# Another order and other buffers for a fused attention and feed-forward block: the feature map's table as the second transfer, its mask first on VectorE, a k weight product ahead of the first transposes

## The chip, the cores and the metric

The kernel runs on one core of one Trainium2 chip. The metric is the time of one execution on the device in microseconds (us). A core has a matrix engine (TensorE, PE in the profile; its weight loads are listed as PEld), three engines for element-wise work (VectorE or DVE, ScalarE or ACT, GpSimd or POOL), and SyncE (SP), which here only issues transfers between the chip's large memory and the on-chip buffers. Each engine takes its instructions strictly in the order in which they were issued to it; engines wait for one another by semaphores.

## What is computed

The input x has 2048 rows of 512. It is normalised, and goes into two branches: linear attention with 32 heads of 16 columns, whose feature map is a product per head followed by a softmax of p and of -p; and a dense layer of 1792, Mish, and a dense layer back. The result is x plus the product of the branches.

```python
def _A_ref(x, wqkv, w_phi, wo):
    ...
    pq = jnp.einsum("bhsd,hdf->bhsf", q, w_phi)
    pk = jnp.einsum("bhsd,hdf->bhsf", k, w_phi)
    phi_q = jnp.concatenate([_softmax(pq, axis=-1), _softmax(-pq, axis=-1)], axis=-1)
    phi_k = jnp.concatenate([_softmax(pk, axis=-1), _softmax(-pk, axis=-1)], axis=-1)
    kv = jnp.einsum("bhsf,bhsd->bhfd", phi_k, v)
    z  = jnp.einsum("bhsf->bhf", phi_k)
    num = jnp.einsum("bhqf,bhfd->bhqd", phi_q, kv)
    den = jnp.einsum("bhqf,bhf->bhq", phi_q, z)[..., None] + 1e-6
    o = num / den
    return (lambda x, *d: x.transpose(*d))(o, 0, 2, 1, 3).reshape(B, S, D) @ wo
...
xn = _layernorm(x, axis=-1)
s = _A_ref(xn, A_wqkv, A_w_phi, A_wo)
g = _silu(_B_ref(xn, B_w1, B_b1, B_w2))
return x + s * g
```

## The kernel before, in words

**Tiles.** The rows of x are cut into 16 tiles of 128 rows, called x0 to x15. `norm` (line 349 and on) loads a tile, takes its mean and variance, raises the variance to the power -1/2 on GpSimd (the result is `rs`), normalises the tile in place, and transposes it on TensorE into a PSUM bank `pt` by four products with the identity. Mean and variance come from VectorE's batch-norm instructions in tiles 0, 1, 4 and 5, and from two passes on ScalarE (the tile is only read, the output goes to a scratch `dev`) in the others.

**Precision.** All large products are made from operands split in two: a high half rounded to the matrix engine's format (`...h`, a copy on ScalarE) and the rest (`...l`, a subtraction on VectorE or GpSimd). A product is three matmuls: high by low, low by high, high by high. Products of weights by tiles are combined by sums of blocks (`sums_x`, `weights_s`, `sums1`), as in fast matrix multiplication, so that seven block products do the work of eight.

**The feature map** is folded into the weights of q and k. Its table `phic` (32 KB) is loaded once; a mask on VectorE spreads it into `phit`, a block-diagonal operand of four 128x128 blocks, and `folded` multiplies each 128 rows of the k weights (loads `wkT00`, `wkT01`, `wkT10`, `wkT11`) and q weights (`wqT..`) by it, four products for each. The products' names are `wkf00` to `wkf11` and `wqf00` to `wqf11`; `wkh`, `wkl` and `wkr` are the halves and a plain copy of a k weight product.

**Stages.** The tiles are normalised and multiplied by the k and v weights (`kx`, `ky`, `kz`, `v`), the softmax of k is taken and summed against v into the bank `kvp`; the first dense layer is the products `fx`, `fy`, `fz` (and `fxq`, `fyq`, `fzq` for q); then the attention's denominators (`tz`), numerators (`pn`) and output (`pw`); then the second dense layer (`x`, `y`, `z`, with Mish on `r`), the products with `md` and `me` last; at the end each tile of the result is put together (`final`) and stored.

**The order is written out by hand.** The functions don't issue instructions; they add them to a list of 2085 operations, numbered as they come (an operation is one instruction, or a group that stays together, such as the four products of `folded`). `Program.issue` then goes through the string `SCHED` and issues them in that order. A letter behind a number chooses the engine where an operation has versions for several: V for VectorE, G for GpSimd, A for ScalarE. The order matters only within each engine's queue, and between instructions that share a buffer. All transfers go to SP's queue, but for the first one in `SCHED`, which ScalarE issues:

```python
g = self.eng["A" if first and m == "dma_start" else e]
first = first and m != "dma_start"
getattr(g, m)(*a, **k)
```

**Buffers.** The string `PLACE` gives each of 985 tiles the number of its buffer within its pool: `slot` (38 large ones), `s2` (15 of 2 KB a partition), `ps` (8 PSUM banks), and small ones. A tile that follows another in the same buffer waits until the last reader of the one before is done; for a load this wait holds SP's queue.

**Numbers used below.** Operations 0 to 10 are eleven products of ones by ones, `wake`, which keep TensorE busy. 25, 155, 36, 366, 168, 240, 64, 379 and 114 load x0, x2, x4, x9, x6, x7, x1, x13 and x5. 11 loads `phic` and 12 is its mask. 13, 14, 15, 16 load `wkT00`, `wkT01`, `wkT10`, `wkT11`, and 17, 21, 56, 60 are the products `wkf00`, `wkf01`, `wkf10`, `wkf11`; 19, 23, 58 and 62 take the low halves of these four, and 63 the copy `wkr1` of the last. 26 to 31 are x0's statistics and normalisation (29 is GpSimd's power), 32 its transposes (`pt0`), 33 and 34 the halves of the result; 37 to 43 are the same for x4, with 42 the normalisation and 43 the transposes (`pt4`). 75 and 76 are the first products `k0`. 107 writes a column of ones. 721, 728 load q weights; 86 and 89 load the v weights. All of them are issued in line 194, so that the profile's groups are told apart by tiles, not by lines.

Of the kernel before, what the change touches and what calls it, by code (L numbers as in the profile page):

```python
# [55 lines left out]
394V 178 733 125V 179 218 395G 137G 389 90 91G 217 735V 219 376 96 353 734A 73 128V 97 253V 377 300 122 98A 143 220 126  # L56
127G 144 93 145 94 134G 221 301 302 186 396 187G 79 390 250 138 194V 99 101 129 123 256V 35 286 287 288 289 251 108 228
95A 109 81 222 146V 147 135 92A 290 130 229 223A 110A 303 230 224 100 78 80 82 131V 136G 262 263A 149 208A 254 304 231V
291 102 225 83 226 255V 139G 190 140G 191A 491 265 193 391 103 112 113G 292 267A 568 523 52 279 148 257 150 104 151 84
85 105 305 306 293 106 195A 258 141 307A 294A 264 192 207 53G 569 281A 210 152 167 188 447 74 142G 196 295 211 308 212  # L60
132 397 570 227 180 613 55 259G 261 197 209V 153 268 296 154 297 321 269 312A 54 189 572 573 313 198 524 525 200 199
448G 309 314G 479 322 452 333 316 354G 315G 450G 356G 357G 651 436 46 480 270 323 334A 336 335 201 202 203 492 493 310
527 338A 311 378 435 398G 351A 232 204 205 503 233 206 271 482 235 273 483 528 355G 484 451G 433 133 260 399 214 213
282 339 284 283 317 318G 285 494A 272 571 504A 656 506 495 274 324V 340 401 234 508A 280A 275 236 341 402 276 298 252
237 496 319 277 497 498 481 238 278 342 358 359G 652G 574 520 522A 413 350 352A 360 414A 505 415 499 416 449G 403 418A
# [36 lines left out]
1426 1577 1198 1199A 1251 1196 1348 1611 1477 1302A 1117 1305A 1259 1457 1260A 1162 1333 1334 1350 1461 1372 1201 1509
1303 1549 1202A 1682 1203 1197 1118 1276 1306 1505 1261 1478 1467 1281 1283 1279 1252 1351 1494 1238 1335 1369 1253
1254 1352 1255 1353 1472 1468 1277 1298 1256 1284 1354 1336 1355 1282 1280 1583 1601 1278 1337 1388 1338 1356 1357 1339
1672 1499 1569G 1683 1673 1340 1385 1257A 1258 1551 1661 1299A 1389A 1511 1662 1376 1534 1674 1550 1663 1584 1684 1386V
1685 1585 1552V 1686 1377 1379 1383 1664 1380 1675 1375 1543 1384 1378 1409 1693 1483 1390 1526 1387 1300 1535G 1469G
1447G 1412 1536G 1687 1665 1676 1440 1381 1688 1382 1436 1200 1677 1473 1474 1520 1553G 1554G 1666 1578 1579 1475 1410V
# [3 lines left out]
1470 1481 1482 1497 1538G 1544 1545 1540V 1603G 1604G 1606G 1506 1635 1501 1594 1507 1765 1525 1529 1502V 1556 1530  # L111
# [832 lines left out]
```

## Time and profile before

| | before |
|---|---|
| timed runs | 485.92 us median of 3 (485.03, 485.92, 491.89) |
| profiled execution, its own time | 484.66 us |
| its span, first to last instruction | 482.9 us |
| mean granted TensorE clock | 0.998 |
| moved by transfers | 112.96 MB, 234 GB/s over the span |

The profile is of one execution. Its span is the time between the first and the last instruction; the own time of the execution is 1.8 us longer. A row of a timeline gives the start, the length, the engine, the line, the operation with output and inputs, and in brackets the idle time before it and what ended that. "xN" counts instructions that were merged into one row; the length of such a row reaches from the first start to the last end. Matmuls are pipelined: a row's last matmul ends later than the next one starts, so that a rate is read from the starts. A product of 32-bit operands appears as two passes, so the four products of `folded` are eight entries.

### The profile page before, as it was taken

Reading aid. Unit: us, or ns where it says so; the run is one execution under the profiler, and the core shown is the slowest. Engines: PE = TensorE matmul, PEld = TensorE weight load, DVE = VectorE, ACT = ScalarE, POOL = GpSimd, SP = SyncE. Lnnn points to the kernel's source line nnn. Section 1 sums busy time; section 2 is a strip of 40 time slices with the busy share of each in tenths; the row PEclk is TensorE's granted clock in tenths of the full one; section 3 lists DMA queues with packets and bytes.
Section 4 is the critical chain, followed back from the end, with each engine's and each line's share of the span. In section 5 each row is a group of like instructions: output and inputs, shape, how many; then the busy total and the mean of one; then the engine's idle time right before and its main releaser. Section 6 shows DMA issues by size and latency. Waiting matters only on the chain.

```text
span 482.9 us, 9043 instructions
## 1 busy us (share of the span) xinstructions
PE 472.5 (98%) x3308; PEld 384.1 (80%) x3308; DVE 444.5 (92%) x749; ACT 316.2 (65%) x534; POOL 248.2 (51%) x168
## 2 busy tenths in 40 slices
PE   6999999999999999999999999999999999999995
PEld 6988888878888888887888877777888888888884
DVE  4999989987999999999999999998899957799985
ACT  6998866754334344435557576598988889976522
POOL 2899948504410084627833365019792627662430
PEclk9999999999999999999999999999999999999999
DMA  8815999674995057994685989985584567621476
GB/s 317 303 37 169 371 331 317 233 260 178 301 342 186 5 185 262 383 297 153 204 282 168 357 325 341 354 306 182 184 260 177 188 210 258 210 102 52 130 244 193
DMA packets 67004, 112.96 MB, mean 234 GB/s; under 512 B 5136, under 2 KB 37520, under 8 KB 66960
## 3 DMA queue, kind: packets, MB, share of 16 engines
q1 hardware_dynamic: 66816, 112.13, 68.6%
q8 instruction: 26, 0.43, 0.3%
q10 hardware_dynamic: 144, 0.26, 0.1%
q14 instruction: 18, 0.15, 0.1%
HBM read 74.62 MB, written 37.75 MB: 233 GB/s over the span
## 4 chain that ended last, share of the span: by engine, by line
PE 97%; DMA 1%; DVE 1%; ACT 1%; issue 0%; POOL 0%; DVEq 0%; ACTq 0%
PE fx L194 16%; PE x L194 16%; PE pw L194 9%; PE kx L194 8%; PE fy L194 8%; PE y L194 8%; PE fxq L194 5%; PE ky L194 4%; PE z L194 4%; PE fz L194 4%; PE kvp L194 2%; PE fyq L194 2%; PE kz L194 2%; PE pn L194 2%; PE pt L194 2%; PE k L194 1%
## 5 line engine op out<-in xcount | busy, mean ns | idle before, releaser
L194 ACT ACTIVATE r<-r,b1t 128x512 f32<-128x512 f32 x56 | 38.9, 717 | 0.6 <-DMA r<-hd 0.6
L194 POOL TENSOR_TENSOR w1al<-w1a,w1ah 128x768 fp32r<-128x768 f32 x9 | 16.8, 1862 | 33.3 <-ACT w1ah L194 31.1
L194 POOL TENSOR_TENSOR w1sl<-w1s,w1sh 128x1024 fp32r<-128x1024 f32 x9 | 21.6, 2411 | 22.7 <-PE kx L194 13.7
L194 POOL TENSOR_TENSOR mt<-r,r 128x512 f32<-128x512 f32 x9 | 13.7, 1522 | 32.8 <-ACT oh L194 18.6
L194 POOL TENSOR_TENSOR t<-r,mt 128x512 f32<-128x512 f32 x9 | 14.9, 1667 | 18.4 <-DVE u L194 12.3
L194 POOL TENSOR_TENSOR rs<-rs,mhalf 128x1 f32<-128x1 f32 x16 | 9.4, 598 | 20.3 <-DVE rs L194 16.5
L194 DVE TENSOR_REDUCE tz<-ez 128x64 f32<-128x1024 f32 x16 | 19.5, 1219 | 0.3
L194 POOL TENSOR_TENSOR tl<-ts,th 128x1024 fp32r<-128x1024 f32 x7 | 16.9, 2416 | 2.4 <-ACT th L194 2.4
L194 ACT ACTIVATE fz<-fx 128x512 f32<-128x512 f32 x14 | 8.2, 582 | 14.9 <-DVE v L194 8.1
L194 PE MATMUL kx<-wss,th 128*128 128x512 f32 x56 | 17.6, 396 | 0.0
L194 POOL TENSOR_TENSOR w1s<-w1a 128x256 f32<-128x256 f32 x16 | 11.9, 748 | 9.7 <-PE fy L194 6.8
L194 ACT ACTIVATE u<-h 128x512 f32<-128x512 f32 x12 | 7.0, 597 | 14.1 <-DVE h L194 14.1
L194 ACT ACTIVATE hd<-fx 128x512 f32<-128x512 f32 x12 | 7.1, 595 | 13.3 <-PE fx L194 13.0
L194 ACT ACTIVATE hc<-fx 128x512 f32<-128x512 f32 x12 | 7.2, 598 | 12.2 <-PE fx L194 12.1
L194 ACT ACT_TABLE_LOAD x11 | 14.1, 1283 | 1.4 <-PEq L936 1.2
L194 POOL TENSOR_TENSOR mt<-r,mt 128x512 f32<-128x512 f32 x9 | 14.8, 1645 | 0.4 <-ACT r L194 0.2
L194 ACT ACTIVATE ha<-fz 128x512 f32<-128x512 f32 x13 | 7.6, 595 | 10.6 <-PE fz L194 5.9
L194 POOL TENSOR_TENSOR md<-t,md 128x512 fp32r<-128x512 f32 x5 | 7.8, 1569 | 11.8 <-ACT md L194 11.8
L194 ACT ACTIVATE hb<-fx 128x512 f32<-128x512 f32 x14 | 8.2, 593 | 8.2 <-PE fx L194 8.2
L194 PE MATMUL pt<-ident,x 128*128 128x128 f32 x64 | 9.9, 287 | 3.2 <-DVE st L194 3.1
L194 PE MATMUL pw<-oh,wo0l 128*128 128x512 f32 x32 | 12.8, 399 | 0.0
L194 PE MATMUL pw<-ol,wo0h 128*128 128x512 f32 x32 | 12.5, 390 | 0.0
(1038 smaller groups left out, 1928.5 us busy)
## 6 DMA issues: line engine op xcount, KB each, us to landing
r<-hd SPq DMA_DIRECT2D x28, 512.0 KB, 5.0
scr<-xT SPq DMA_DIRECT2D x8, 512.0 KB, 6.6
scrT<-th SPq DMA_DIRECT2D x8, 512.0 KB, 7.0
scrT<-tl SPq DMA_DIRECT2D x8, 512.0 KB, 6.3
so<-so SPq DMA_DIRECT2D x16, 256.0 KB, 4.0
sr<-so SPq DMA_DIRECT2D x16, 256.0 KB, 4.5
xx<-xt SPq DMA_DIRECT2D x16, 256.0 KB, 4.1
x<-x SPq DMA_DIRECT2D x15, 256.0 KB, 4.1
```

What stands on the lines that cost most here:

```text
L194: getattr(g, m)(*a, **k)
```

## The change

Only the two strings `SCHED` and `PLACE` change. Every operation is kept, and three get another engine: 42, the normalisation of x4 (ScalarE to VectorE), 107, a column of ones (ScalarE to VectorE), and 1756, the low half `md3l` (GpSimd to VectorE).

At the start, by queue:

| queue | before | after |
|---|---|---|
| transfers | x0 (by ScalarE); SP: x2, x9, wkT11, phic, x4, x7, x6, x1, wkT00, wkT01, x13, wqT00, wqT01, x5, wqT10, wkT10, wv | x2 (by ScalarE); SP: x0, phic, wkT11, x9, x4, wkT10, x6, x7, wkT00, x1, x13, wkT01, wqT00, wqT10, x5, wqT01, wv |
| PE | 6 wake, pt0, wkf11, 3 wake, pt4, 2 wake, wkf00, wkf01, pt2, wqf00, pt6, wqf10, wkf10, pt1, wqf01, k0 | 6 wake, wkf11, pt0, wkf10, 3 wake, pt4, 2 wake, wkf00, pt2, wkf01, wqf00, wqf10, pt6, wqf01, pt1, k0 |
| VectorE | x0 statistics, rs0, x0 normalised, (x9), mask, (x9, x2), x4 statistics, rs4, wkr1, ... | x0 bn_stats, mask, (x2), bn_aggr, rs0, x0 normalised, (x9), x4 statistics, rs4, (x2, x9), wkr1, (x6, x2), x4 normalised, ... |
| ScalarE | x2, x9, x2, x9, xT0 high half, x7, x6, x4 normalised, wkf11 high half, ... | x2, x2, x9, x9, x6, xT0 high half, wkf11 high half, x7, ... |

On VectorE the low halves 19, 23 and 58 of k weight products each go ahead of other work, and the normalisations of x7 and x13 come behind 23 and 58. On GpSimd the sum `ws2` of weights goes ahead of `ws0`.

Behind that, TensorE's queue has two moves: 928 (a product of `fx10`) goes ahead of 774, and 1691 (a product of `x0_0`) ahead of 1703. Some 40 instructions of the other queues move by a few places. At the end, on SP, the store 2072 of a quarter of tile 11 goes ahead of the store 2022 of tile 12, and the two halves of tile 10 change places.

Of the 985 tiles most get another buffer number, but 76 follow another tile than before in their buffer; about half of these lie in the head, up to the first k and v products. Those that hold a load: wkT10 has a buffer of its own (before: behind wkT11), wkT01 follows the scratch of x2's passes (before: its own), x13 follows phic (before: its own), x5 follows x0 (before: phic), and x10 follows wkT00 (before: wkT01).

```diff
--- before.py
+++ after.py
@@ -48,76 +48,76 @@
 SCHED = """
-25 26 27 28 29 155 156 157 0 1 2 3 4 5 30 31V 32 366 367 159 16 11 368 12 36 370 369 158 33 37 160 371 38 39 40 41 60 6
-7 8 240 168 64 13 14 63V 379 241 169 161 162 170 42A 61 172 372 242 65 171 34 43 9 10 17 243 163V 21 164 720 721 114
-728 722 47A 244 15 48 66 173 174 67 62 18 380 175 373 245 176V 68 24A 107A 20A 724A 69 382 115 49G 381 51 19 116 177
-383 723A 181A 22 730 56 57 165 44 732A 374A 246 50G 384 70V 385 247 117 89 86 248V 23 386 387V 184G 118 71 725 727A
-731A 58 166 478 215 75 729 76 299 59V 119 182 45 77V 726V 183V 388 249 375 111G 87 88G 120A 121 392A 393 185 72 216
...
+155 25 26 11 156 12 157 159 27 28 29 30 31V 0 1 2 3 4 5 16 60 366 367 368 32 36 15 56 37 38 39 40 370 158 168 169 33
+371 63V 369 41 240 171 160 6 7 8 42V 43 13 64 379 14 161 170 34 65 162 61 241 242 172 720 728 372 9 10 243 163V 17 114
+164 47A 244 721 48 66 173 174 107V 67 62 380 18 175 373 245 176V 68 20A 21 24A 381 383 722 724A 382 69 19 49G 51 115
+723A 22 730 177 181A 57 165 44 732A 374A 246 50G 384 70V 116 385 247 89 86 23 117 386 248V 58 387V 184G 118 725 71 727A
+731A 166 478 215 75 729 76 299 59V 119 182 45 77V 726V 183V 388 375 87 137G 111G 88G 120A 733 121 392A 393 185 72 216
...
-880 888 774 777 980 887 928 1035 1060 842 1018 929A 881 782 889 1061 1036 1062 1064 882 930 783 890 852G 853 1019 1037
...
+819G 922 833 877 771 834 950 750 797 946 947 977G 925 940 941 927 747 966 923A 926A 928 929A 879 835 978 1016 886 979
...
-1732 1670 1746 1716 1717 1712G 1718 1738 1733 1719 1720 1721 1681 1692 1703 1691 1714 1747 1723V 1725 1702 1713 1724
+1732 1670 1716 1717 1712G 1718 1746 1738 1733 1719 1720 1721 1681 1692 1691 1747 1723V 1703 1714 1725 1702 1713 1724
...
-1742G 1735G 1878 1801 1766 1767 1760 1796V 1790 1768 1726 1802 1869 1820 1756G 1761 1728 1772 1850 1900 1862 1797 1839
+1742G 1735G 1878 1801 1766 1767 1760 1796V 1790 1768 1726 1802 1869 1820 1756V 1761 1728 1772 1850 1900 1862 1797 1839
...
-2050 1981 2023 2018 2024 2045G 1978 2019 2020 2025 2026 2068 2010 2016 2051 1985 2027 2028 2065 2034 2066 2081 2082
-1986 2073 2069 2077 2070 2083 2084 2074 2021 2075 2022 2071 2078 2079 2080 2072 2076 2037 2040 2043 2046 2049 2052 2053
-2056 2057 2054 2055 2058 2059
+2050 1981 2018 2023 2024 2045G 1978 2019 2020 2025 1985 2026 2068 2010 2016 2051 2027 2028 2065 2034 2066 2081 2082
+1986 2073 2069 2077 2070 2083 2084 2074 2021 2075 2071 2072 2022 2078 2079 2080 2076 2037 2040 2043 2046 2049 2056 2057
+2052 2053 2058 2059 2054 2055
 """
 PLACE = """
-0 6 7 3 12 13 5 5 9 8 11 4 5 0 0 0 1 0 2 1 8 7 3 8 14 9 3 4 6 17 20 1 2 7 1 2 11 13 6 15 23 19 4 5 10 3 5 16 20 21 15
...
+0 2 4 3 13 3 9 5 9 8 11 5 7 1 1 0 2 0 3 2 8 4 3 5 14 8 4 9 6 17 19 1 2 7 3 1 14 13 5 15 24 20 0 7 3 3 4 16 19 22 15 27
...
```

More of the change, by code (lines that the diff above doesn't have):

```diff
@@ L56 @@
[L56 to L65, printed above, removed]
@@ new lines @@
+93 145 94 134G 221 186 396 187G 79 390 250 138 194V 99 123 101 129 256V 35 286 287 288 289 251 108 228 95A 300 301 302
+109 81 222 146V 147 135 92A 130 229 223A 110A 303 230 224 100 78 290 80 225 82 131V 136G 262 263A 149 208A 254 304 231V
+291 102 83 226 255V 139G 190 140G 191A 491 265 193 391 103 112 113G 292 267A 568 523 52 279 148 257 150 104 151 84 85
+105 305 306 293 106 195A 258 141 307A 294A 264 192 207 53G 569 281A 210 152 167 188 447 74 142G 196 295 211 308 212 132
+397 570 227 180 613 55 259G 261 197 209V 153 268 296 154 297 321 269 312A 54 189 572 573 313 198 524 525 200 199 448G
@@ new lines @@
+309 314G 479 322 452 333 316 354G 315G 450G 356G 357G 651 436 46 480 270 323 334A 336 335 201 202 203 492 493 310 527
+338A 311 378 435 398G 351A 232 204 205 503 233 206 271 482 235 273 483 528 355G 484 451G 433 133 260 399 214 213 282
+339 284 283 317 318G 285 494A 272 571 504A 656 506 495 274 324V 340 401 234 508A 280A 275 236 341 402 276 298 252 237
+496 319 277 497 498 481 238 574 575 278 342 358 359G 652G 520 522A 413 350 352A 360 414A 505 415 499 416 449G 403 418A
+266A 509 454 529 430 526 344 239 343 510 654G 345 500 325 419 511 653G 453G 655G 434 530 124 549 658 445 442 444 362
@@ new lines @@
+364 441 327 326 657G 363 365 404A 420 659G 614 615 501 789 421 617 432A 328 502 660 400 406 405 455G 661 346 407 616
+347 348 550 662 551 552 408 663A 329 460 361G 330 331 337V 555 438 664 443 576A 553A 417A 409 461 665 521V 349 422 485
+618 332 619 486V 760V 620 556A 531A 465 462 759V 463A 457 487 459 456 532 554 423 425 410 458 424 411 533 558 666A 466A
+559A 668 446 440 437 507A 464 320 426 439 562 621A 488 536A 669V 412 431A 468 672 537 427 673A 469A 622 538V 540 489
+545 546 577 578 472 467 626V 539V 534 535 627 629G 579 563V 628V 470 630 541 542G 473A 631 623 632G 580 490 564 761V
@@ L76 @@
+639 640 475 476 512 557 624 428 429 581 667 692 582 583 641 513 515 514 516 670 560 633 634 693A 593 695 471 543 477
+625 678 786G 785G 762G 517 584A 586 518 519 642A 644 585 646 643 587 645 787G 788G 791 594A 595 675 647 790G 676 588
+680 589 544 596 565 648 548 547 635 636 598V 599 610 694 566 590 591 679 681 688 686 697A 709 612V 698 699 649 736 600
+592 650 700 611V 737 687 690 684 689 685 861 792G 765 738 862 863 701 601 603 605 602 703 604 864 739A 711A 606 865
 866A 696A 597A 638 713 637 712 702 741 953 704 705 607 608 955 706 609 952 710V 707 793 868 867 742A 869A 743 954 677
@@ L77 @@
 691 872 683 682 870 871 708 794 798 799A 744 956 745A 986 987 988 873 989 714 957 958 715 716 717 719 718 801 746 756
-994 996 995 990 991 758A 754A 992 763 874 751 875 876 752 755 764G 800 748 961 757V 802V 795 805 767 997 806A 749V 803
-960 963 820 811 1002G 766G 813G 1003 962 804 671 753 943 938 740 561 768 998 772 993 999 1004 1005 1001 964 821 816 769
+994 996 995 990 991 758A 754A 992 763 874 751 875 876 752 755 764G 800 748 961 757V 802V 795 805 767 997 806A 803 749V
+960 963 820 811 1002G 766G 813G 1003 962 804 671 753 943 938 561 768 998 772 993 999 1004 1005 1001 964 821 816 769
@@ L95 @@
-1230G 1244 1421A 1418A 1392 1329 1092 1107 1156 1186 1396 1361A 1532 1322 1314 1157 1342 1096 1341 1187 1397A 1033
+775 776A 828A 920 840 921 779 826 831 809 674 740 807 567 796A 780A 818 1010 841 829 1013 1014 830 832 885 878 1015
+819G 922 833 877 771 834 950 750 797 946 947 977G 925 940 941 927 747 966 923A 926A 928 929A 879 835 978 1016 886 979
+1137 1262 1017 880 888 774 777 980 887 1035 1060 842 1018 881 782 889 1061 1036 1062 1064 882 930 783 890 852G 853 1019
+1037 932 1039 1063 1038 949 843 902G 948 924 945 951 1065A 883 981 982 845 983 854 935 933A 1267 891 892 984 855 903
@@ new lines @@
+884 904 844 847 856 1086 846 1040A 781 810 944 942 474 1051 931 784 1067 1042 1119 1043A 1046 1120 1139G 1138G 1268G
+905 1263G 1140G 911G 1141G 857 959 858 985 906 1085 1047 1068A 848 1124 1071 1125A 1127 1142 1128A 1052G 907 908 849
+909 912 936 913 1088 1087 1121 910 1122A 1123 1265G 1264G 1143G 1054G 1126 1131 1132A 1056 778 934 1147 1072 914 1146
+915 1320 1144 1089 1145G 1266G 1269 1057G 1066 1041 1044 859 1069 1045 1271 1048 1073 1204 916 1129 1148 1149 1049 917
+1150 1074 1050 1130 1134 1135 1151 1205 1316 937 1133 1163 1053G 1075 918 1209 1055G 1058 1136 1566 1321 1272 1164 1165
@@ new lines @@
+1059G 1273 1206 1210A 1166A 1207A 1270G 1285 1222 1239 1324 1223 919 1274A 1240 1325 893G 968G 1326 1168 1169A 1241 894
+1224 850 895 1225 969 1212 1152 1171 1286A 1288 1317 1213A 1216 1211 896 970 1153 1172A 971 1327 1226 1567 1217A 1182
+851 1242 972 1175 1070 1170 1287 1176A 1289A 1292 1090 1091 1318 1184 1181 1167 1311 1310 1313 1319 1243 1328 1415 1173
+1214 1183 973 1219 897 1103 1290 1105 974 898 1178 975 1102 1177 1220 899 1179 1416 1295 1420 1358 1154G 1032 1312 1315
+1275 1093G 1323 1180 1293A 1568 1185 1294 1221 1359 900 1417 1391 1360 1363 1155 1227 1104 1106 1174 1094 1296 1095
@@ L96 @@
+1230G 1244 1421A 1342 1418A 1392 1329 1092 1107 1156 1186 1396 1361A 1532 1322 1314 1157 1096 1341 1187 1397A 1033
 1189G 1393 1394A 1097 1343 1098 1229 1344 1158 1398 1423 1419 1218 1362 1020 1215 1208 1399 1228 1424A 1400A 1345 1364A
@@ L98 @@
 1404A 1488 1110G 1291 1108 1476 1425 976 1406 1233 1407 1076 1111 1234 1112 1081 1082 1430 1431 1235 1370 1077 1083
-1079 1365 1084 1113 1078 1236 1021 1371A 1465 1023 1034G 1349G 1332G 1080 1114 1368 1346 1237 1190 1030 1489 1026 1456
+1079 1365 1084 1113 1078 1236 1021 1371A 1465 1023 1349G 1332G 1034G 1080 1114 1368 1346 1237 1190 1030 1489 1026 1456
 1022G 1455 1027 1031 1024 1450 1191 1429 1660 1395 1432 1402 1443 1297 1498 1373 1307 1247G 1248 1192 1246 1028 1249
 1115 1250 1374 1029 1193 1533 1445 1444 1330 1446 1347 1466 1116 1025 1194 1101 1195 1301 1304 1308A 1600 1671 1649
[L102 to L105, printed above, removed]
+1426 1577 1198 1199A 1251 1348 1611 1477 1302A 1117 1305A 1259 1457 1260A 1162 1333 1334 1196 1350 1461 1372 1201 1509
+1303 1549 1467 1202A 1682 1203 1197 1118 1276 1306 1505 1478 1281 1283 1279 1252 1351 1494 1261 1238 1335 1369 1352
+1253 1254 1255 1353 1472 1468 1277 1298 1256 1284 1354 1336 1355 1282 1280 1583 1601 1278 1337 1388 1338 1356 1357 1339
+1672 1534 1499 1569G 1683 1673 1340 1385 1257A 1258 1551 1661 1299A 1389A 1511 1662 1376 1674 1550 1663 1584 1684 1386V
 1685 1585 1552V 1686 1377 1379 1383 1664 1380 1675 1375 1543 1384 1378 1409 1693 1483 1390 1526 1387 1300 1535G 1469G
-1447G 1412 1536G 1687 1665 1676 1440 1381 1688 1382 1436 1200 1677 1473 1474 1520 1553G 1554G 1666 1578 1579 1475 1410V
+1447G 1412 1536G 1687 1665 1553G 1676 1440 1381 1688 1382 1436 1200 1677 1473 1474 1520 1554G 1666 1578 1579 1475 1410V
 1462 1650 1651 1413V 1414 1634 1612 1441 1463 1464 1613 1523 1580 1652 1437A 1521A 1451 1571V 1570G 1572G 1442 1653
```

26 lines of the change are left out of this document (2 added, 24 removed), and 40 rows, old and new, of the table PLACE.

## The prediction

> **What bounds the kernel now.** I read the page first: the busy times and the chain that ended last.
>
> ```profile
> span 482.9 us, 9043 instructions
> PE 472.5 (98%) x3308; PEld 384.1 (80%) x3308; DVE 444.5 (92%) x749; ACT 316.2 (65%) x534; POOL 248.2 (51%) x168
> ...
> PE 97%; DMA 1%; DVE 1%; ACT 1%; issue 0%; POOL 0%; DVEq 0%; ACTq 0%
> ```
>
> TensorE (PE) is busy for 472.5 of 482.9 us and carries 97% of the chain. The change neither removes nor adds a matmul, so all that it can win lies in the 10.4 us in which PE stands still. Next the view of what PE waited for, longest first, and the table by stage (after the length of the stage: PE, weight loads, DVE, ACT, POOL).
>
> ```profile
> PE pt L194 <- DVE st L194: 3.1, 1, 3.1
> PE wake L194 <- DVE mhalf L276: 1.1, 1, 1.1
> PE fx L194 <- issue: 1.0, 1, 1.0
> ```
>
> ```profile
> 11.00:18.50 7.50, 7.50 (x69) 7.43 (x68) 7.50 (x29) 7.50 (x21) 5.09 (x8) 1.00 1.02 361
> 18.50:30.00 11.50, 11.50 (x64) 9.67 (x64) 11.47 (x30) 11.47 (x25) 11.07 (x7) 1.00 0.40 137
> 30.00:478.00 448.00, 446.81 (x3149) 360.78 (x3148) 419.15 (x666) 289.68 (x475) 228.74 (x142) 1.00 0.69 234
> 478.00:483.00 5.00, 0.00 (x0) 0.00 (x0) 1.43 (x4) 0.58 (x2) 0.00 (x0) 0.80 0.36 100
> ```
>
> From 30 to 478 us PE stands still for 448.00 - 446.81 = 1.2 us, of which 1.0 is the one stop of fx that no engine explains ("issue"). The last 5 us have no matmul. The prize is the head, where the first tile's transposes wait 3.1 us.
>
> **The head, row by row.** The PE timeline (start, length, operation; the idle time before it in brackets), and one piece of the chain with eight passes further on:
>
> ```profile
> 1.12 2.93 PE L194 MATMUL wake<-ones 128*128 128x128 f32 x12 [1.12 <-DVE mhalf L276]
> 7.13 1.09 PE L194 MATMUL pt<-ident,x 128*128 128x128 f32 x4 [3.08 <-DVE st L194]
> 8.01 1.92 PE L194 MATMUL wkf<-phit,wkT 128*128 128x128 f32 x8
> 9.71 0.96 PE L194 MATMUL wake<-ones 128*128 128x128 f32 x6
> 10.82 0.66 PE L194 MATMUL pt<-ident,x 128*128 128x128 f32 x4 [0.15 <-ACT x L194]
> ...
> 38.24 0.48 PE L194 MATMUL kx<-wss,tl 128*128 128x512 f32 x1
> ```
>
> ```profile
> 16.38 0.89 PE wkf L194 x8
> ```
>
> PE is idle from 4.05 to 7.13. The k weight product then needs 9.71 - 8.01 = 1.70 us for eight passes that take 0.89 at 16.38: the array steps at half speed. The six passes at 9.71 take 0.96, about one slow and five fast ones, so half speed ends near 9.9. VectorE (DVE) in the same stretch:
>
> ```profile
> 4.54 0.69 DVE L194 BATCH_NORM_STATS2 st<-x 128x6 f32<-128x512 f32 x1 [3.47 <-DMA x<-x]
> 5.27 0.18 DVE L194 BATCH_NORM_AGGREGATE mv<-st 128x2 f32<-128x6 f32 x1
> ...
> 6.31 0.21 DVE L194 TENSOR_SCALAR nb<-mv,rs 128x1 f32<-128x1 f32 x1 [0.61 <-POOL rs L194]
> 6.44 0.54 DVE L194 TENSOR_SCALAR x<-x,mv,rs 128x512 f32<-128x512 f32 x1
> ...
> 6.96 0.68 DVE L194 TENSOR_TENSOR phit<-phic,bmask 128x512 f32<-128x512 f32 x1
> 7.56 0.21 DVE L194 TENSOR_SCALAR mv<-st 128x1 f32<-128x1 f32 x2
> ...
> 9.44 0.21 DVE L194 TENSOR_SCALAR nb<-mv,rs 128x1 f32<-128x1 f32 x1 [0.67 <-POOL rs L194]
> ...
> 9.96 0.69 DVE L194 COPY wkr<-wkf 128x512 f32<-128x512 f32 x1 [0.31 <-PE wkf L194]
> ```
>
> GpSimd's pow for rs, ScalarE's normalising of x4, and SP's issues of x9, wkT11 and phic:
>
> ```profile
> 8.85 1.59 POOL L194 TENSOR_TENSOR rs<-rs,mhalf 128x1 f32<-128x1 f32 x3 [2.57 <-DVE rs L194]
> ```
>
> ```profile
> 9.97 0.80 ACT L194 ACTIVATE x<-x,nb,rs 128x512 f32<-128x512 f32 x1
> ```
>
> ```profile
> 1.25 0.42 SPq L194 DMA_DIRECT2D x<-x  x1
> 1.72 0.42 SPq L194 DMA_DIRECT2D wkT<-wqkT  x1
> 2.18 0.43 SPq L194 DMA_DIRECT2D phic<-phi  x1
> ```
>
> Last the transfers' time from issue to landing: wkT11, phic, and x6, the slowest of the first eight.
>
> ```profile
> wkT<-wqkT SPq DMA_DIRECT2D x1, 256.0 KB, 4.0
> phic<-phi SPq DMA_DIRECT2D x1, 32.0 KB, 3.7
> x<-x SPq DMA_DIRECT2D x1, 256.0 KB, 4.7
> ```
>
> So wkT11 is there at 1.72 + 4.0 = 5.72 and the table phic at 2.18 + 3.7 = 5.88, though its mask runs only at 6.96.
>
> **The change part by part.**
>
> Transfers. phic moves to SP's second place (issue 1.25), past x9 and wkT11: it lands at 1.25 + 3.7 = 4.95; the bound from above is 1.25 + 4.7 = 5.95. wkT11 keeps its issue time, so 5.72. x2 and x0 change places between ACT's and SP's queue; both were issued first on their queue, so I take 0. wkT10 gets a buffer of its own and goes ahead of x6, x7 and wkT00: SP issues one transfer per 0.47 us, so it leaves near 3.1 and lands by 7.8 at x6's 4.7. In exchange wkT01's load waits behind ScalarE's second pass over x2, and x5's behind the transposes of x0 (buffers reused), and what stands behind them on SP (wqT01, the v weights) waits too. Before, wkT10's own load held SP until the k product at 8.01 was done; so I take 0.
>
> Mask first. It stands between bn_stats (the next row starts at 5.27) and bn_aggr. It costs 7.56 - 6.96 = 0.60 us there, so x0's chain, and with it pt0, moves from 7.13 to 7.73. Queued behind it are x0's rs, for which GpSimd's pow waits, x0 itself, and the mean for ScalarE's second pass over x2.
>
> k product ahead of the first transposes. phit is ready at 5.27 + 0.60 = 5.87 and wkT11 at 5.72, so wkf11 starts near 6.0 instead of 8.01, takes its half-speed 1.70 us to 7.7, and pt0 follows at 7.73 without a gap. PE's idle time shrinks from 7.13 - 4.05 to 6.0 - 4.05: a gain of 1.13 us. wkf10 (at 16.38 before) now follows pt0: 0.89 us of real work that keeps PE fed until x4 is there.
>
> x4 on VectorE. Before, ScalarE reached it at 9.97, though rs4 had come at 9.44, and pt4 started at 10.82. By VectorE's rows x0 now ends near 7.5, bn_stats of x4 near 8.2, and its rs leaves at 8.5; one pow takes 1.59 / 3 = 0.53, and the fillers now ahead (the 0.6 us copy wkr1 among them) end at 9.5. x4 takes 0.45 (6.96 - 6.44, less a small one) and is ready at 10.0. PE comes to pt4 after pt0 (7.73 + 0.88), wkf10 (0.9 to 1.7) and three wake products (0.67), at 10.2 or later, so the wait of 0.15 us goes. Sum: 1.13 + 0.15 = 1.28 us.
>
> The clock takes some of it back. Two bounds: half speed ends 2.8 us after PE starts again (7.13 to 9.9), as before, and nothing is lost; or it ends at 9.9 whatever PE does, and 6.0 to 7.13 is run at half speed in addition, which loses 0.56 us and leaves 0.72. Nothing in one trace tells these apart, so I take the middle, 1.0. [...]
>
> Does the lead survive? ScalarE loses x4 (0.80) and a small copy, so it gains. VectorE loses the waits 0.61, 0.67 and 0.31, gets one of about 0.65 for x0's pow with no mask to fill it, and takes 0.45 + 0.1 on: 0.4 us ahead. It is without a gap from 11 to 30 us (7.50 of 7.50, 11.47 of 11.50), so it keeps 0.4 where PE has 1.0; I cost that at nothing because the low halves of the k weights, which k0 reads, each move ahead of a normalisation of 0.54. GpSimd is tight once:
>
> ```profile
> 35.35 2.45 POOL L194 TENSOR_TENSOR wss<-ws,wss 128x1024 fp32r<-128x1024 f32 x1
> ```
>
> It ends at 37.8, and PE's second pass after 38.24 (near 38.5) reads it: 0.7 us of slack for a lead of 1.0. If GpSimd gained nothing, 0.3 us would be lost; its chain starts with the v weights, which come earlier, so I take 0.
>
> The rest. Behind its first 31 groups PE's order differs in two places (928 and 1691, each one group earlier). Some 40 moves on the other queues shift an instruction by a few places; md3's low half goes from GpSimd to VectorE, and at the end the halves of tile 10 swap and the store of a piece of tile 11 overtakes tile 12's. I cost each at nothing: from 11 to 478 us no engine holds PE. If one cover fails, the price is that of one instruction, 0.5 to 2.4 us (the x and wss rows). The last 5 us stay.
>
> Sum: the profiled execution took 484.66 us (span 482.9) and would take 483.7. The timed runs are 485.03, 485.92 and 491.89, so the profiled one lies 1.3 below their median. I start from 485.5, between the two lower ones, and forecast 484.5.
>
> **Rivals.**
> 1. VectorE becomes the bound of the head. For: no gap from 11 to 30 us, and x4 on top. Against: PE has never waited for it there. Gain 0.4, or nothing if x0's pow finds no filler: 485.1 to 485.5.
> 2. The mask waits for its table: slower. VectorE's queue is in order, so a late phic holds x0, its pow, pt0 and SP's later loads. If VectorE also sets the pace with its lead of 0.4, the time gets longer once phic lands later than 5.27 + 0.4 = 5.7, that is 4.4 us after issue. At x6's 4.7 it is 5.95 and costs 0.3 us: 485.8. Against: 3.7 with four transfers ahead of it on SP and ACT; now there are two.
> 3. The stop of 1.0 us goes too, since nothing in the trace ties it to the order: 483.5. It may as well come a second time.
> 4. The moved buffers and places give a new wait in the long middle: one instruction, 0.5 to 2.4 us, less the gain: slower, 485.0 to 486.9.
>
> **How the numbers follow.** Forecast (0.7 to 1.3 us gained) 0.5; rival 1 0.2; rival 2 0.08; rival 3 0.07; rival 4 0.15. The predicted time is the forecast's 484.5. Low end: 485.03 - 1.28 - 1.0 = 482.8, the whole head and the stop from the lowest run; high end: 485.5 + 2.4 - 1.0 = 486.9, rival 4 at its largest. About what a measurement of this kernel can tell from no change is 2%, 9.7 us; PE's whole idle time is 10.4, of which the last 5 and the first 1.1 stay. Faster by over 2%: 0.01; slower by over 2% needs several new waits of the largest size: 0.02; within 2%: 0.97.
>
> **What would show it.** In the changed profile PE's first long wait should end near 6.0 after 1.9 us, with wkf ahead of pt, and pt0 near 7.7; VectorE's mask at about 5.3 with no wait for a transfer; x4 on VectorE near 9.5; pt4 at 10.2 to 10.9 with all second k weights multiplied; and the kx that started at 38.24 near 37.2. The pass times of the head tell the clock. The sum is wrong if that kx comes at 38 or later, the mask if its row waits for a DMA, and "the rest" if PE's waits after 40 us are longer than the 1.0 of before.

## The result, and the profile after

The changed kernel takes 490.04 us, the median of 20 runs (488.35 to 491.73), beside 486.66 us of the kernel before in the same runs: a ratio of 1.0057, 95% interval 1.0037 to 1.0077. That is slower by 0.6%, within the 2% at which a run counts as the same, but on the other side of the forecast and above its range. Some executions of the kernel before, and of several others below, are 1 to 1.5% longer than the rest of the same kernel; the ratios leave out only those that lie over 1.5% above the kernel's fastest, so medians and ratios both still carry a part of them.

The page of the changed kernel. Its profiled execution took 490.19 us:

```profile
span 488.4 us, 9048 instructions
PE 473.9 (97%) x3308; PEld 383.5 (79%) x3308; DVE 449.4 (92%) x752; ACT 315.2 (65%) x532; POOL 247.2 (51%) x167
...
PE 88%; DVE 7%; issue 2%; DMA 1%; ACT 1%; SPq 1%; DVEq 0%; ACTq 0%
```

TensorE is busy for about as long as before (473.9 against 472.5 us); the span is 5.5 us longer. The medians differ by less, 3.4 us, because the profiled execution before took 484.66 us, 2.0 us under its kernel's median. The chain that ended last now has 7% on VectorE, where it had 1%. The view of what PE waited for says where (total, times, longest):

```profile
PE fx L194 <- issue: 1.9, 1, 1.9
PE wkf L194 <- DVE st L194: 1.9, 1, 1.9
PE x L194 <- DVE ma6l L194: 1.3, 1, 1.3
PE wake L194 <- DVE mhalf L276: 1.1, 1, 1.1
PE pt L194 <- DVE x L194: 1.0, 1, 1.0
PE v L194 <- DVE xT L194: 0.6, 1, 0.6
PE pt L194 <- DVE wkr L194: 0.5, 1, 0.5
PE wqf L194 <- DVE xT L194: 0.4, 1, 0.4
```

Of these only the stop of fx and the two first waits of the head have a counterpart before; the five others are new, and all five are for VectorE. The table by stage (length, then PE, weight loads, DVE, ACT, POOL, granted clock), first of the changed kernel, then of the one before where its rows were not shown:

```profile
18.50:30.00 11.50, 9.65 (x53) 7.64 (x52) 11.50 (x24) 9.45 (x20) 10.61 (x6) 1.00 0.37 136
30.00:42.00 12.00, 11.37 (x53) 9.03 (x52) 11.90 (x25) 10.82 (x22) 11.46 (x8) 1.00 0.06 23
42.00:300.00 258.00, 255.53 (x2204) 205.97 (x2203) 247.89 (x421) 143.73 (x236) 131.08 (x87) 1.00 0.76 255
300.00:478.00 178.00, 176.73 (x883) 142.60 (x882) 159.10 (x219) 136.01 (x219) 85.77 (x49) 1.00 0.63 210
```

```profile
30.00:42.00 12.00, 12.00 (x55) 9.70 (x55) 11.83 (x24) 10.91 (x22) 12.00 (x7) 1.00 0.12 45
42.00:300.00 258.00, 256.98 (x2209) 207.60 (x2209) 248.50 (x424) 145.06 (x237) 130.26 (x87) 1.00 0.77 260
300.00:478.00 178.00, 177.83 (x888) 143.48 (x886) 158.82 (x220) 133.71 (x219) 86.48 (x49) 1.00 0.62 208
```

PE's idle time is length less busy. From 18.5 to 30 us it is 1.85 us (0 before), from 30 to 42 us 0.63 (0), to 300 us 2.47 (1.02), to 478 us 1.27 (0.17): 5.0 us more in all, beside the 5.5 us between the spans. Nearly 1 us of it, in the stage to 300 us, is the stop of fx, which no engine explains.

The first 18 us went nearly as planned. From the timelines of PE and VectorE of the changed kernel:

```profile
5.91 2.08 PE L194 MATMUL wkf<-phit,wkT 128*128 128x128 f32 x8 [1.86 <-DVE st L194]
7.78 1.06 PE L194 MATMUL pt<-ident,x 128*128 128x128 f32 x4
...
10.62 0.66 PE L194 MATMUL pt<-ident,x 128*128 128x128 f32 x4
...
17.93 0.50 PE L194 MATMUL k<-wkh,xT 128*128 128x512 f32 x1
...
40.94 0.48 PE L194 MATMUL kx<-wss,tl 128*128 128x512 f32 x1
```

```profile
5.18 0.67 DVE L194 TENSOR_TENSOR phit<-phic,bmask 128x512 f32<-128x512 f32 x1
```

The mask stands at 5.18 without a wait for a transfer, wkf11 at 5.91, pt0 at 7.78, and k0 at 17.93 (18.45 before): 0.5 us ahead where 1.0 was forecast. But the kx that should have come near 37.2 comes at 40.94, 2.7 us later than before. Three rows of VectorE and the GpSimd (POOL) rows beside them show the loss: x13's normalisation, the copy of ones into v5's extra columns, and `tl1`, the low half of a sum of tiles that kx reads. The changed kernel first:

```profile
19.25 2.52 DVE L194 TENSOR_SCALAR x<-x,mv,rs 128x512 f32<-128x512 f32 x1
...
32.01 1.65 DVE L194 COPY v<-ones 128x16 f32<-128x16 f32 x1
...
40.81 1.91 DVE L194 TENSOR_TENSOR tl<-ts,th 128x1024 fp32r<-128x1024 f32 x1
```

```profile
19.11 2.38 POOL L194 TENSOR_TENSOR ws<-wkr,wvr 128x1024 f32<-128x1024 f32 x1
...
31.21 2.41 POOL L194 TENSOR_TENSOR ws<-ws,wkr 128x1024 f32<-128x1024 f32 x1
...
41.59 3.39 POOL L194 TENSOR_TENSOR ws<-wkr,ws 128x1024 f32<-128x1024 f32 x1
```

The same three and their GpSimd neighbours before:

```profile
18.39 0.54 DVE L194 TENSOR_SCALAR x<-x,mv,rs 128x512 f32<-128x512 f32 x1
...
29.88 0.31 DVE L194 COPY v<-ones 128x16 f32<-128x16 f32 x1
...
37.44 1.45 DVE L194 TENSOR_TENSOR tl<-ts,th 128x1024 fp32r<-128x1024 f32 x1
```

```profile
18.75 2.46 POOL L194 TENSOR_TENSOR ws<-wvr,wvr 128x1024 f32<-128x1024 f32 x1
...
30.09 2.46 POOL L194 TENSOR_TENSOR ws<-ws,wkr 128x1024 f32<-128x1024 f32 x1
...
35.35 5.81 POOL L194 TENSOR_TENSOR wss<-ws,wss 128x1024 fp32r<-128x1024 f32 x2
```

Read starts and ends together. Before, the normalisation starts 0.36 us ahead of GpSimd's sum and takes 0.54; after, it starts 0.14 us behind one, takes 2.52, and ends at 21.77, 0.3 us behind the end of the sum (21.49). The copy of 128x16 elements starts 0.21 us ahead of a sum and takes 0.31; after, it starts inside one, takes 1.65 and ends with it. These two make VectorE 1.98 + 1.34 = 3.3 us late, and tl1 starts 3.4 us later than before; tl1 itself, blocked for a while in both kernels, adds only 0.5. In the other direction, before, tl1 gets in at the end of the first of two GpSimd instructions, and the pair takes 5.81 us instead of twice 2.4. The loser doesn't run slower, it stands still until the winner is done: in the six profiles of this kernel and of the runs below in which the copy starts inside the sum, it starts 0.1 to 0.9 us behind the sum's start and always ends 0.02 to 0.04 us behind its end. The prediction did not weigh this.

### The profile page after: what moved, and what is told of

Its sections match the earlier page's. It is cut to its first block, busy times and chain, and to the rows that moved or that the text cites. A ratio compares the mean times of both kernels' runs of the same rounds, so it can differ in the third digit from the quotient of the medians.

```text
span 488.4 us, 9048 instructions
## 1 busy us (share of the span) xinstructions
PE 473.9 (97%) x3308; PEld 383.5 (79%) x3308; DVE 449.4 (92%) x752; ACT 315.2 (65%) x532; POOL 247.2 (51%) x167
## 4 chain that ended last, share of the span: by engine, by line
PE 88%; DVE 7%; issue 2%; DMA 1%; ACT 1%; SPq 1%; DVEq 0%; ACTq 0%
PE fx L194 16%; PE x L194 15%; PE pw L194 9%; PE fy L194 8%; PE y L194 8%; PE kx L194 7%; PE fxq L194 4%; PE ky L194 4%; PE fz L194 4%; PE z L194 3%; PE fyq L194 2%; PE kvp L194 2%; PE pn L194 2%; PE kz L194 1%; DMA x<-x 1%
## 5 line engine op out<-in xcount | busy, mean ns | idle before, releaser
L194 POOL TENSOR_TENSOR mt<-r,r 128x512 f32<-128x512 f32 x9 | 12.7, 1408 | 35.7 <-ACT oh L194 18.6
L194 POOL TENSOR_TENSOR w1s<-w1a 128x256 f32<-128x256 f32 x16 | 11.7, 740 | 10.2 <-PE fy L194 7.1
L194 PE MATMUL fx<-ft3h,w1ah 128*128 128x512 f32 x28 | 10.9, 389 | 1.9 <-issue 1.9
L194 POOL TENSOR_TENSOR md<-t,md 128x512 fp32r<-128x512 f32 x4 | 6.5, 1638 | 11.8 <-ACT md L194 11.8
L194 PE MATMUL pw<-oh,wo0h 128*128 128x512 f32 x32 | 12.5, 390 | 0.0
```

## The experiments

Two theories stood against each other. **Blocking:** the head's new order lets VectorE instructions start inside GpSimd's long sums (or ask at a moment when GpSimd wins), and each GpSimd instruction that one of them stands behind costs up to 2.4 us. **Load, or the rest:** VectorE has too much work, or the moves behind 50 us cost the time. The results in one table: the ratio is to the kernel before in the same runs with its 95% interval; then, from the one profiled execution, the span, how long the three VectorE instructions took (x13, v5, tl1), and PE's wait for tl1, all in us. A span is about 1.8 us shorter than the time of its execution, which can lie some us off the median: it took 491.40 us in run 7 (median 488.36) and 486.52 in run 10 (median 490.97).

| run | median | ratio | span | x13 | v5 | tl1 | PE's wait for tl1 |
|---|---|---|---|---|---|---|---|
| before | 486.7 to 487.4 | 1 | 482.9 | 0.54 | 0.31 | 1.45 | none |
| after | 490.04 | 1.0057 [1.0037, 1.0077] | 488.4 | 2.52 | 1.65 | 1.91 | 0.2 |
| 1 changed head, old rest | 491.02 | 1.0046 [1.0009, 1.0083] | 489.7 | 2.53 | 1.65 | 2.70 | 0.9 |
| 2 old head, changed rest | 486.20 | 0.9969 [0.9920, 1.0018] | 482.9 | 0.54 | 0.33 | 1.45 | none |
| 3 after, x13 moved back | 489.89 | 1.0038 [0.9996, 1.0081] | 489.7 | 0.53 | 2.37 | 3.84 | 2.2 |
| 4 before, x13 moved behind 58 | 489.21 | 1.0054 [1.0030, 1.0078] | 487.3 | 2.44 | 1.54 | 1.43 | none |
| 5 run 3, v5 on ScalarE | 490.97 | 1.0078 [1.0042, 1.0114] | 490.5 | 0.54 | 0.22 (ACT) | 5.25 | 3.4 |
| 6 after, ws2 moved back | 488.05 | 1.0024 [1.0005, 1.0043] | 487.2 | 2.53 | 1.64 | 2.74 | 0.9 |
| 7 before, v5 one place later | 488.36 | 1.0046 [1.0015, 1.0078] | 489.7 | 0.54 | 1.88 | 4.47 | 2.5 |
| 8 run 5, tl1 two places up | 487.39 | 1.0019 [0.9977, 1.0062] | 485.0 | 0.54 | 0.22 (ACT) | 1.93 | none |
| 9 before, tl1 one place later | 488.88 | 1.0050 [1.0014, 1.0086] | 486.7 | 0.54 | 0.26 | 3.17 | 1.4 |
| 10 run 8, ma6l ahead of mb1l | 490.97 | 1.0054 [1.0007, 1.0101] | 484.6 | 0.53 | 0.22 (ACT) | 1.91 | none |
| 11 as run 2 | 484.58 | 0.9956 [0.9942, 0.9971] | 482.9 | 0.54 | 0.31 | 1.42 | none |

**1 and 2: which part of the change.** The first 400 operations of the string come from one kernel, the rest from the other; the buffers follow.

```diff
 SCHED = """
-25 26 27 28 29 155 156 157 0 1 2 3 4 5 30 31V 32 366 367 159 16 11 368 12 36 370 369 158 33 37 160 371 38 39 40 41 60 6
+155 25 26 11 156 12 157 159 27 28 29 30 31V 0 1 2 3 4 5 16 60 366 367 368 32 36 15 56 37 38 39 40 370 158 168 169 33
...
```

> The changed order and buffers up to the 400th operation (about 50 us), the old ones behind. Theory A (the time is lost in the head, where the normalisation of x13 now starts while GpSimd sums ws2 and takes 2.5 us for 0.5): 2 to 3.5 us over before, and PE's first product of wss near 41 us as in the changed kernel (38.2 before). Theory B (the moved places and buffers behind the head cost it): 0.7 us under before to equal. Theory C (both): 1 to 2 us over before.

> The old order and buffers up to the 400th operation, the changed ones behind: the complement of the run on the head. Theory A: within 0.7 us of before. Theory B: 2 to 3.5 us over before, with a long VectorE instruction near 360 us (ma6l took 2.49 us there for 1.40 before). Theory C: 1 to 2 us over before.

The head alone makes the kernel slower (1.0046) and shows the same three long rows; the rest alone does not (0.9969, and none of the rows). So the loss is the head's, though a part of it, PE's wait of 1.1 to 1.3 us for ma6l (a low half in the second dense layer, blocked in the same way: in the changed kernel it starts at 363.00, inside GpSimd's mb2l of 361.02 to 364.41, and takes 2.49 for 1.40 before), shows only at 360 us.

**3 and 4: the swap of x13's normalisation with the low half 58.** One token moves, in the changed kernel back, in the kernel before forward:

```diff
-... 248V 58 387V 184G 118 725 71 727A
+... 248V 387V 58 184G 118 725 71 727A
```

```diff
-... 248V 23 386 387V 184G 118 71 725 727A
-731A 58 166 478 ...
+... 248V 23 386 184G 118 71 725 727A
+731A 58 387V 166 478 ...
```

> The changed kernel with one swap in VectorE's queue: x13's normalisation (387) back ahead of the low half wkl1 (58), so that it starts about 0.6 us earlier, before GpSimd's sum ws2. Theory A: the normalisation takes 0.54 us again, PE's first product of wss comes at 37.5 to 39 us, and the time falls by 2 to 3.5 us from the changed kernel, to before or up to 0.7 us under it. Rival (VectorE is simply the bound of the head, with x4 added to it): the swap moves nothing, time within 0.7 us of the changed kernel.

> The kernel before with the same swap the other way: 387 behind 58, nothing else. Theory A: 387 starts near 19.0 us inside GpSimd's sum (18.75 to 21.2 before) and takes some 2.2 us; PE waits at the transposes behind it; 1 to 3 us over before. Rival: two neighbours in VectorE's queue change places, within 0.5 us of before.

Run 4 came out as blocking said: the normalisation starts at 19.76, 0.25 us behind GpSimd's sum, takes 2.44, and the kernel before loses 0.5% by this one swap. VectorE, late by it, then comes into the next sum with the copy (1.54), and PE waits 1.4 us for ma6l in this run too.

```profile
19.76 2.44 DVE L194 TENSOR_SCALAR x<-x,mv,rs 128x512 f32<-128x512 f32 x1
```

```profile
19.51 2.40 POOL L194 TENSOR_TENSOR ws<-wvr,wvr 128x1024 f32<-128x1024 f32 x1
```

Run 3 did not: the normalisation is cured (0.53), and the time stays at 489.89. The theory that this one instruction makes the loss fell. The rows of run 3 show why: VectorE now arrives at the copy of ones 0.09 us after GpSimd's ws1, and later tl1 takes 3.84 us: it asks 0.4 us before the end of the second wss, but GpSimd's next sum, ws3, gets in ahead of it, and PE waits 2.2 us for it:

```profile
30.45 2.37 DVE L194 COPY v<-ones 128x16 f32<-128x16 f32 x1
```

```profile
30.36 2.44 POOL L194 TENSOR_TENSOR ws<-ws,wkr 128x1024 f32<-128x1024 f32 x1
```

**5: the copy of ones off VectorE.** Run 3 with one letter changed:

```diff
-93 145 94 134G 221 186 396 187G 79 390 250 138 194V 99 123 101 129 256V ...
+93 145 94 134G 221 186 396 187G 79 390 250 138 194A 99 123 101 129 256V ...
```

> The changed kernel with x13's normalisation ahead of the low half (as in the run before) and, besides, the copy of ones into v5 on ScalarE in place of VectorE. That copy took 2.37 us on VectorE at 30.5 us, inside GpSimd's ws1, against 0.31 undisturbed. Theory (VectorE and GpSimd shut each other out for a whole instruction): the copy on ScalarE is done in about 0.2 to 0.3 us, VectorE is 2.0 us earlier behind it, and tl1 then starts near 37.9 instead of 40.0 us, beside the end of GpSimd's wss0 (38.0), so that it takes either about 1.4 or about 3.5 us; the time falls by 1.0 to 2.5 us from 489.9, to 487.4 to 488.9, or to about 486 if tl1 goes free too. Rival (the lateness comes from VectorE's amount of work, and the long rows are a symptom): the time stays within 0.5 us of 489.9.

The copy takes 0.22 us on ScalarE and VectorE is 1.8 us earlier at tl1, as expected, but the time did not fall: 490.97 lies above what the theory and what the rival gave. Until tl1 PE was level with the kernel before (kx on wss at 38.41 against 38.24). Then tl1 stood behind two GpSimd instructions, and PE stood for 3.4 us; the rows of VectorE, GpSimd and PE, and the stage behind:

```profile
38.14 5.25 DVE L194 TENSOR_TENSOR tl<-ts,th 128x1024 fp32r<-128x1024 f32 x1
```

```profile
35.25 4.75 POOL L194 TENSOR_TENSOR wss<-ws,wss 128x1024 fp32r<-128x1024 f32 x2
...
39.96 2.35 POOL L194 TENSOR_TENSOR ws<-wkr,ws 128x1024 f32<-128x1024 f32 x1
```

```profile
43.44 0.50 PE L194 MATMUL kx<-wss,tl 128*128 128x512 f32 x1 [3.40 <-DVE tl L194]
```

```profile
44.00:47.00 3.00, 3.00 (x8) 2.31 (x7) 3.00 (x7) 0.91 (x2) 0.00 (x0) 0.50 0.06 16
```

tl1 asks at 38.14, half a microsecond into the second of the two wss (37.61 to 40.00), waits for it, loses to ws3 at 39.96 and runs when that ends at 42.31. The last row's granted clock is 0.50: behind the stop PE started about eight passes 0.43 us apart instead of 0.23, so the stop cost some 1.6 us more than its length.

**6: GpSimd's order or VectorE's.** The changed kernel with ws2 back behind ts9:

```diff
-... 183V 388 375 87 137G 111G 88G 120A 733 121 392A 393 185 72 216
-394V 178 125V 179 218 395G 389 90 91G ...
+... 183V 388 375 87 111G 88G 120A 733 121 392A 393 185 72 216
+394V 178 125V 179 218 395G 137G 389 90 91G ...
```

> The changed kernel with one token moved: GpSimd's ws2 back behind ts9, as before the change; VectorE's order is untouched. Theory (what counts is that x13's normalisation starts on VectorE after a long GpSimd sum has started): it takes about 2.5 us again, now beside ws0 in place of ws2, and the time stays at 489.5 to 490.5. Rival (the new order on GpSimd with ws2 first is what costs): the normalisation takes 0.54 us and the time falls to 487 to 488.

The normalisation is blocked for just as long, now by ws0 (it starts at 18.98, the sum at 18.83): whether the normalisation is blocked depends on VectorE's place relative to any long sum, not on which sum it is. The time is not the theory's: 488.05 lies 1.4 us below its range and 0.05 above that of the rival (the new order on GpSimd costs), so that a price of GpSimd's order is not excluded. In this run ma6l was not blocked and PE did not wait for it, which would be 1.3 of the 2.0 us gained; the rest is open.

**7 and 9: one blocked instruction in the kernel before.** In 7 the copy of ones moves behind the reduction that follows it, in 9 tl1 behind the sum that follows it:

```diff
-... 250 138 194V 99 101 129 123 256V ...
+... 250 138 99 194V 101 129 123 256V ...
```

```diff
-... 224 100 78 80 82 131V 136G 262 263A 149 208A 254
+... 224 100 78 80 82 136G 262 263A 149 131V 208A 254
```

> The kernel before with one pair swapped on VectorE: the copy of ones into v5 (0.31 us, at 29.88 us, just ahead of GpSimd's ws1 at 30.09) behind the reduction that follows it. It then starts near 30.5, inside ws1 (30.09 to 32.55). Theory: this copy of 128x16 elements takes 1.9 to 2.2 us, VectorE is 1.7 us late behind it, and the time rises by 0.5 to 2.5 us from 487.0. Rival (so small a copy does not need what GpSimd holds, or the delay is absorbed): 0.31 us, or the time within 0.3 us of 487.0.

> The kernel before with one pair swapped on VectorE: tl1, which starts there at 37.44 us, 0.3 us before GpSimd's wss2 (37.72), behind the sum of k1 of 0.67 us. It then starts near 38.1 us, 0.4 us after wss2. Theory: tl1 takes 3.3 us (one GpSimd instruction) or 5.3 us (two), GpSimd's wss2 takes 2.4 us in place of 3.4, TensorE waits 1.5 to 3.5 us for tl, and the time rises by 1.5 to 4.5 us from 487.0, though no work is added and the lead of the first transfers plays no part. Rival (the slack ahead of kx1 absorbs it): the time stays within 0.5 us of 487.0.

Both as blocking said, and neither adds work or touches the first 28 us. In 7 the copy starts inside ws1, takes 1.88 us, VectorE comes late to tl1, which then takes 4.47; PE waits 2.5 us for it:

```profile
30.75 1.88 DVE L194 COPY v<-ones 128x16 f32<-128x16 f32 x1
```

```profile
30.19 2.42 POOL L194 TENSOR_TENSOR ws<-ws,wkr 128x1024 f32<-128x1024 f32 x1
```

In both runs PE also waits 1.3 us for ma6l, as in the changed kernel. In 9 tl1 takes 3.17, GpSimd's two wss 2.4 each (4.78 together, against 5.81 before, where tl1 got in between), and PE waits 1.4 us for tl1:

```profile
38.80 3.17 DVE L194 TENSOR_TENSOR tl<-ts,th 128x1024 fp32r<-128x1024 f32 x1
```

```profile
36.12 4.78 POOL L194 TENSOR_TENSOR wss<-ws,wss 128x1024 fp32r<-128x1024 f32 x2
```

**8: tl1 ahead of GpSimd.** Run 5 with tl1 moved up by two instructions of VectorE:

```diff
-... 303 230 224 100 78 290 80 225 82 131V 136G 262 263A 149 ...
+... 303 230 224 100 131V 78 290 80 225 82 136G 262 263A 149 ...
```

> The kernel of the run with the ones on ScalarE, with tl1 moved two places up on VectorE, ahead of the reduction and the sum of k0. There TensorE had no lag behind the kernel before until tl1 (0.00 us at the q product after the v loads), and tl1, which started at 38.15 us, half a microsecond after GpSimd's wss2 (37.61), took 5.25 us over two GpSimd instructions; TensorE then lagged by 5.4 us. [...] Theory (tl1 alone makes what is left of the loss): it takes 1.2 us from the end of wss0, some 2.0 in all, GpSimd's wss2 takes 3.4 us, TensorE's wait for tl falls from 3.4 us to under 0.5 us, and the time falls by 2.5 to 4.5 us from 491.0, to 486.5 to 488.5. Rival (tl1 loses again at the end of wss0, or the next instruction is blocked in its stead): the row of tl1 stays above 4 us, or the time stays above 489.

```profile
36.60 1.93 DVE L194 TENSOR_TENSOR tl<-ts,th 128x1024 fp32r<-128x1024 f32 x1
```

```profile
35.03 5.78 POOL L194 TENSOR_TENSOR wss<-ws,wss 128x1024 fp32r<-128x1024 f32 x2
```

tl1 wins between the two wss, as in the kernel before, and the row, the wait and the time (487.39) all lie where the theory put them. PE's wait for tl1 and the slow passes behind it are gone, the span falls from 490.5 to 485.0 us, and the time to about that of the kernel before (1.0019 [0.9977, 1.0062]). Of the 5.5 us between the two spans, 3.4 are the stop and 1.6 the slow passes. The intervals of the two ratios just overlap, so it is the traces that show it. Not all of the head's loss is cured: run 11 below, with the same rest and the old head, is at 0.9956, and PE still waits 1.2 us for ma6l and 0.6 for x0's transposes here.

**10: the wait at 360 us.** Run 8, there with two more pairs swapped:

```diff
-... 1696 1547 1557V 1562 1508 1513V 1514 1515 ...
+... 1696 1547 1562 1508 1513V 1557V 1514 1515 ...
-... 1516V 1699 1518V 1574G 1537G 1628 ...
+... 1516V 1699 1518V 1537G 1574G 1628 ...
```

> The kernel of the run with tl1 moved up, and near 357 us two more swaps: on VectorE mb1l (2.14 us there, 1.22 undisturbed) behind ma6l (2.50, 1.40 undisturbed), which the x product waits 1.2 us for; on GpSimd mb2l behind r1_0's sum. Theory: ma6l asks for the port at 358.0 us, gets it when r1_0's sum ends near 358.8, is done by 360.1, TensorE's wait of 1.2 us for it falls to under 0.3 us, and the time falls by 0.7 to 1.4 us from 487.4, to 486.0 to 486.7. Rival (the wait moves to the next of these instructions, mb1l or mb2l): the time stays within 0.4 us of 487.4.

No run shows a port. What the rows show in its place: the copy of ones (six profiles), x13's normalisation and tl1, started inside a long GpSimd instruction, end only behind the end of that one, or, as tl1 in the runs 3, 5 and 7, of the next. PE's wait for ma6l went, but mb1l behind it took 3.41 us beside mb2l, and PE then waited 0.9 us for h and 0.5 for w2x. The wait moved to the next instruction, as the rival had it. The time fits neither: the median of 490.97 lies 3.6 us above that of run 8, and the trace, of an execution of 486.52 us, doesn't show why (its span is 484.6, against 485.0 in run 8).

**11: the rest of the change once more.**

> The kernel with the order before the change in the first 50 us and the changed order behind it, once more: its ratio was 0.9969 [0.992, 1.0018]. Theory (the change's rest is worth something, and the head loses it): a ratio of 0.994 to 0.998 again. Rival (the rest is worth nothing): 0.999 to 1.002.

The ratio is 0.9956 [0.9942, 0.9971]: the moves and buffers behind 50 us are worth 0.4%, 2 us, and with the old head in front they beat both kernels. Where the 2 us lie is open: the profiled execution has the span of the one before, 482.9 us, but that one lies 2.0 us under its kernel's median.

## Why the prediction was wrong, step by step

- **Transfers, mask first, k product ahead, x4 on VectorE: right.** Mask at 5.18 with no DMA wait (said 5.3), wkf11 at 5.91 (6.0), pt0 at 7.78 (7.7), pt4 at 10.62 (10.2 to 10.9). x4's normalisation came at 10.03, 0.5 us later than said; pt4 starts 0.05 us behind its end, still in the range.
- **The clock takes half back, 1.0 us left: the size came out on the average, in part by luck.** The granted clock reads 1.00 all through the head in the traces of both kernels, so "half speed" is read from the passes alone (eight passes of wkf in 1.70 us from 8.01 on, 0.89 from 16.38 on, both before). k0 starts at 17.84 us in the mean of the seven profiles with the changed head (17.40 to 18.36) and at 18.80 in the mean of the six with the old one (18.45 to 19.34). The single pair of before and after shows 0.5. Two of the six old ones are late (19.34 and 19.32, runs 4 and 9) because the passes there stay at half speed to about 12.6 us (in run 4 four `wake` passes take 0.85, before 0.45; in run 9 all 22 are busy for 5.3 us, before for 4.5); without these two the lead is 0.7. In the changed kernel half speed ends near 9.0 us, since the eight passes of wkf10 from 8.63 take only 1.09: that is between the two bounds, 8.7 and 9.9. The end moves from run to run, in runs 4 and 9 far beyond both.
- **The sum's start: too low.** It began at 485.5, from two of three runs; the median of twenty is 486.66. Of the 5.5 us between the forecast and the measured time, 1.2 lie there, 1.0 is the gain that was forecast, and 3.4 are the loss.
- **"Does the lead survive?": the step that failed.** It priced VectorE by its gaps and costed the swaps at nothing "because the low halves of the k weights, which k0 reads, each move ahead of a normalisation of 0.54". The row of 0.54 was true only where no GpSimd sum was running when the instruction started. The swap of 58 and x13 put that normalisation 0.14 us behind a GpSimd sum and it took 2.52 us; run 4 shows that the swap alone costs 0.5%.
- **Its second half failed too: "GpSimd is tight once".** The 0.7 us of slack of wss were looked at as a question of when the data are there. What mattered was who starts first, and at the copy and at x13 0.1 to 0.4 us decided that: with the swap undone (run 3) VectorE and GpSimd still stand otherwise to each other than before, by 0.3 us at the copy, and the copy and tl1 lost.
- **The rest, at nothing: wrong in sign, small in size.** The runs 2 and 11 give a gain of 0.3 to 0.4%. The check named for it misled: PE's waits after 40 us did grow (ma6l 1.3, fx 1.9), but not by the rest. The wait for ma6l is absent in runs 2 and 11, which have the changed rest, and present in runs 4, 7 and 9, which have the old one and a single swap in the head; how a shift in the head reaches 360 us no run traces. The stop of fx tells nothing: it is between 0.2 and 1.9 us in the thirteen profiles, with either head (1.1 and 1.4 in runs 2 and 11).
- **The rivals.** The first, VectorE as the bound of the head, had the right engine and the wrong reason and price: VectorE got only three instructions more (752 against 749); its standing still is new. The second did not come: the mask did not wait for its table. Nor did the third: the stop of fx was longer (1.9). The fourth had the right price for one instruction, 0.5 to 2.4 us, but placed it in the long middle, and one alone; the long rows were two in the head (x13 and the copy), with tl1 a little longer, and two near 360 us (mb1l 2.26 for 1.22, ma6l 2.49 for 1.40), of which PE waited for the second.

## What to carry to other kernels

Here VectorE and GpSimd were both nearly without gaps (busy for 11.47 and 11.07 of 11.50 us from 18.5 to 30 us before), and the time of a VectorE instruction could not be taken from its own row: look at which GpSimd instruction runs when it starts, and treat the 0.54 of this case as "0.54, or the rest of GpSimd's 2.4". A gain of a few tenths at the start was worth less here than the order of the two engines at their next meetings, and a cure at one meeting has to be followed to the next one until PE no longer waits.

## What the hardware showed that was not expected

- A copy of 128x16 elements took 0.31 us, or 1.5 to 2.4 us inside a GpSimd sum. Statistics on 128x1 and instructions that read a PSUM bank, in the same stretches, kept their 0.14 and 0.68 us (in the changed kernel inside GpSimd's tl, 34.09 to 36.49: st at 36.02 in 0.14, xT at 34.17 in 0.68).
- Who gets in at the end of a GpSimd instruction is not only a matter of who asked first. In all thirteen profiles tl1 asks while a GpSimd instruction runs. In ten it gets in when that ends, having asked 0.3 to 2.1 us ahead; in runs 3, 5 and 7 it asked 0.4, 1.9 and 1.1 us ahead and lost to ws3, against which it won in five others. What decides this is open.
- Stops of PE of 2.2, 2.5 and 3.4 us (runs 3, 7, 5) were each followed by seven or eight passes of 0.43 us instead of 0.23, in run 3 at a granted clock of 0.57 and in run 5 of 0.50 (44 to 47 us); one of 1.4 us (run 9) was not (1.00 from 42 to 45 us). The length of one stop alone does not decide it: in the profiles of runs 1 and 6 the granted clock is 0.50 for some 3 us from 24 us on (their means over the span are 0.995 and 0.994, that of the changed kernel 0.998), behind stops of 0.9, 0.5 and 0.4 us within 3.5 us, while the changed kernel, with the same three stops (1.0, 0.5 and 0.4), shows 1.00 there.
